# Moving the gate factors, the diagonals and a zeroing in an attention and two-layer MoE kernel

## The chip, the core and the metric

The kernel runs on one core of a Trainium2 chip. The metric is device time in microseconds; the kernel before has a median of 632.36 us over 3 runs (630.68 to 632.56).

## What is computed

Inputs are q, k, v of 2 batches, 8 heads, 576 positions and 64 features, all float32. Three stages follow each other.

```python
# 1. attention with 128 positive random features
phi(x) = exp(x @ omega.T - |x|^2/2 - max) / sqrt(128)
num = phi(q) @ (phi(k).T @ v);  den = phi(q) @ sum(phi(k)) + 1e-6
x = (num / den), heads side by side            # 1152 x 512
# 2. top-1 mixture of 8 experts (512 -> 1024 -> 512)
e_idx = argmax(x @ w_gate);  gate_w = softmax(x @ w_gate)[e_idx]
eom = sigmoid(x @ w_output_gate)
out[row] = gate_w * eom[e_idx] * (relu(x @ w1[e_idx]) @ w2[e_idx])
# 3. dense mixture of 4 experts, weights p = domain_probs / sum
out = sum_e p[:, e] * (relu(out @ w1[e]) @ w2[e])
```

## The kernel before

Float32 products are made of three matmuls each: an operand is split into a rounded high part (a cast on ScalarE, L91) and the remainder (a subtraction, L92, on VectorE or GpSimd), and high x high, high x low and low x high are summed (`mm3`, lines 594 to 596).

*Attention* (lines 506 to 577) is a software pipeline over banks: for each batch b, half hh of the heads, and kind k or q. Stage A transposes (L273), stage B projects into a PSUM bank `pj` (L295 to L297), takes maxima (L300), makes the bias `nb` (L304, L305) and the exponentials `e` (L312, ScalarE). Stage C for k multiplies into `kv` (L326), which shares a PSUM bank with the maxima; for q it transposes `e` (L357). Stage D (`stage_d`, L365) divides (`rd`, `xn`: L377 to L380), writes `xn` to memory for later (L382), transposes (L385) and writes `xh` (ScalarE, L396) and `xl` (VectorE, L397). The tiles of one half are j = 0 to 3 and then the remaining 64 rows.

*Gate.* When a batch's last half is done, `gate_logits` (L400) makes the logits of both gates in two column groups: `lgs` (ScalarE copy, L411) and `lgr`, the 32 remaining columns (VectorE copy, L412). `gate_tr` transposes them (L418); `main_expert` finds the batch's most frequent expert: `gm_eq` (L431), a count matmul (L433), and `ei`. `gate_math` (L449) makes the factors of every row: exponentials on ScalarE (L463, L465) and sixteen small VectorE operations (L459 to L487). `gate_count` (L489) counts rows by expert and chunk with two matmuls and a VectorE sum `cnt`.

*First mixture.* The 1152 rows are four chunks of 288 columns, two a batch. A chunk's main expert is applied to all its rows: layer 1 (`unit1`, eight PSUM tiles `ph`) and layer 2 (`unit2_blocks`, four blocks of 24 matmuls into `py`). A row's factor is zero when its expert is another. The factors come in through `gate_row` (L620): three diagonal pieces `dg` (128x128 twice, 128x32) are spread over partitions by a matmul with ones (L627). The other pairs of expert and chunk that have rows are listed by `extras` (L689); one of them with at most 64 rows is gathered, computed and added in packed form (lines 758 to 848, "the pair": `mask`, `rank`, `og`, `ogf`). Any others would run in a loop (L853). `x2T`, the result, is written by chunks 0 and 1 and added to by chunks 2 and 3, whose columns are therefore zeroed first (L755, GpSimd).

*Second mixture* (lines 885 to 1063) takes the time from about 260 us on: all four experts for all rows, with weights streamed in and split on ScalarE and GpSimd.

*Order.* The program is written in one sequence. A planner then builds each engine's queue from modelled times: whatever is ready and stands earliest in the program goes next. So an instruction can be queued far ahead of its place in the program. On the chip each engine executes its queue in order, and semaphores carry the dependences. `tc.issue_after(ins)` adds an order edge to `ins` for those instructions of its block that run on the same engine as `ins`; instructions on other engines get no edge. Before the change the factors of both batches stand in the program behind layer 1 of chunk 0 (L674), and the planner queues most of batch 0's into the attention of batch 1.

Of the kernel before, what the change touches and what calls it, by code (L numbers as in the profile page):

```python
# [12 lines left out]
AF = mybir.ActivationFunctionType  # L13
ALU = mybir.AluOpType
# [11 lines left out]
NC = 288  # L26
# [14 lines left out]
def moe_stack(ctx, tc, q, k, v, omega, w_gate, w_ogate, mw1, mw2, dprobs, dw1, dw2, out):  # L41
    nc = tc.nc
    TT, STT, TS = nc.vector.tensor_tensor, nc.vector.scalar_tensor_tensor, nc.vector.tensor_scalar

    def f32(ap):
        return ap.bitcast(F32)
# [8 lines left out]
    ps_n = ctx.enter_context(tc.tile_pool(name="ps_n", bufs=2, space=PSUM))  # L55
# [6 lines left out]
    ident = cp.tile([128, 128], F32, name="ident")  # L62
# [13 lines left out]
    fold = cp.tile([128, 32], F32, name="fold")  # L76
# [7 lines left out]
    lgr = cp.tile([16, 128], F32, name="lgr")  # L84
# [280 lines left out]
    def stage_d(b, hh, u):  # L365

        t = st_e["T", u]
        rest = u[1] == 2
        m = 64 if rest else 128
        c0 = 64 * b if rest else 0  # L370
        bank = ps_n.tile([128, 512], F32, tag="nd", name="pnd")
        ps = bank[:, 0:G * (D + 1)].rearrange("p (g d) -> p g d", g=G)
        for i in range(G):
            nc.tensor.matmul(ps[:m, i, :], t[:, i, c0:c0 + m], kvs[b, hh][:, i, :], start=True, stop=True)

        rd = ap.tile([128, G], F32, tag="rd", name="rd", bufs=4)
        TS(rd[:m], ps[:m, :, D], M * 1e-6, None, op0=ALU.add)  # L377
        nc.vector.reciprocal(rd[:m], rd[:m])
        xn = ap.tile([128, G, D], F32, tag="xn", name="xn", bufs=4)
        TT(xn[:m], ps[:m, :, 0:D], rd[:m].unsqueeze(2).to_broadcast([m, G, D]), op=ALU.mult)  # L380
        dst = xs[8, 64 * b:64 * b + 64] if rest else xs[4 * b + SLOT_J[u[3]]]
        nc.sync.dma_start(dst[:, 256 * hh:256 * hh + 256], xn[:m].rearrange("p g d -> p (g d)"))  # L382
        px = bank[:, 0:256].rearrange("p (g n) -> p g n", g=2)
        for g in range(2):
            nc.tensor.transpose(px[:, g, :m], xn[:m, 2 * g:2 * g + 2, :].rearrange("p a d -> p (a d)"), ident[:m, :m])  # L385
        kbs = slice(2 * hh, 2 * hh + 2)
        if rest:
            cols = slice(S * b, S * b + S)
            dh, dl = (z[:, kbs, cols].rearrange("p k (c n) -> p k c n", c=2)[:, :, :, 256:NC] for z in (xh, xl))
            src = px[:, :, 0:64].rearrange("p k (c n) -> p k c n", c=2)  # L390
        else:
            s = SLOT_J[u[3]]
            col = S * b + NC * (s // 2) + 128 * (s % 2)
            dh, dl = (z[:, kbs, col:col + 128] for z in (xh, xl))
            src = px
        nc.scalar.copy(dh, src)  # L396
        TT(dl, src, f32(dh), op=ALU.subtract)  # L397


    def gate_logits(b, psp, tag):  # L400
        lgs = cp.tile([16, 4, 128], F32, tag="lgs", name="lgs")
        for c in range(2):
            ps = psp.tile([16, NC], F32, tag=tag, name="lgp")
            cc = 2 * b + c
            mms = []
            for kb in range(KB):
                for a, x in ((wgh, xh), (wgh, xl), (wgl, xh)):
                    mms.append((a[:, kb, :], x[:, kb, NC * cc:NC * cc + NC]))
            for i, (a, x) in enumerate(mms):
                nc.tensor.matmul(ps, a, x, start=i == 0, stop=i == len(mms) - 1)  # L410
            nc.scalar.copy(lgs[:, 2 * c:2 * c + 2, :], ps[:, 0:256].rearrange("p (t n) -> p t n", n=128))  # L411
            nc.vector.tensor_copy(lgr[:, 32 * cc:32 * cc + 32], ps[:, 256:NC])  # L412
        return lgs

    def gate_tr(b, lgs, psp, tag):
# [33 lines left out]
    def gate_math(b, lg, mx, eq, m, cb):  # L449

        l, z = lg[:, :, 0:NE], lg[:, :, NE:2 * NE]

        def sm(nm, n=NE):
            return cp.tile([128, 5, n] if n > 1 else [128, 5], F32, tag="gm_" + nm, name="gm_" + nm)

        def bc(a):
            return a.unsqueeze(2).to_broadcast([128, 5, NE])

        TS(ohb[:, b], cb, m[:, 0:1], None, op0=ALU.is_equal)  # L459
        d = sm("d")  # L460
        TT(d, l, bc(mx), op=ALU.subtract)
        p = sm("p")
        nc.scalar.activation(p, d, AF.Exp)  # L463
        sg = sm("sg")
        nc.scalar.activation(sg, z, AF.Exp, scale=-1.0)  # L465
        w = sm("w")
        TT(w, eq, rev.unsqueeze(1).to_broadcast([128, 5, NE]), op=ALU.mult)
        wm = sm("wm", 1)
        nc.vector.tensor_reduce(wm, w, axis=AX.X, op=ALU.max)
        oh = sm("oh")  # L470
        TT(oh, w, bc(wm), op=ALU.is_equal)
        ss = sm("ss", 1)
        nc.vector.tensor_reduce(ss, p, axis=AX.X, op=ALU.add)
        TS(ss, ss, 1e-9, None, op0=ALU.add)
        nc.vector.reciprocal(ss, ss)
        TT(p, p, bc(ss), op=ALU.mult)
        TS(sg, sg, 1.0, None, op0=ALU.add)
        nc.vector.reciprocal(sg, sg)
        TT(p, p, sg, op=ALU.mult)
        r = slice(64 * b, 64 * b + 64)  # L480
        nc.vector.tensor_copy(oh_all[:, 4 * b:4 * b + 4, :], oh[:, 0:4])
        TT(g_all[:, 4 * b:4 * b + 4, :], p[:, 0:4], oh[:, 0:4], op=ALU.mult)

        cs = slice(2 * b, 2 * b + 2)
        cm = cmask[:, cs].unsqueeze(2).to_broadcast([128, 2, NE])
        TT(ohr[:, cs], oh[:, 4:5, :].to_broadcast([128, 2, NE]), cm, op=ALU.mult)
        TT(grm[:, cs], p[:, 4:5, :].to_broadcast([128, 2, NE]), ohr[:, cs], op=ALU.mult)  # L487

    def gate_count(b, psp, tag):  # L489
        ps = psp.tile([128, 2, 3, NE], F32, tag=tag, name="cps")  # L490
        nc.tensor.matmul(ps[:, :, 0:2], ones, oh_all[:, 4 * b:4 * b + 4, :].rearrange("p (c t) e -> p c t e", t=2),
                         start=True, stop=True)
        nc.tensor.matmul(ps[:, :, 2], ones, ohr[:, 2 * b:2 * b + 2], start=True, stop=True)
        nc.vector.tensor_reduce(cnt[:, 2 * b:2 * b + 2], ps.rearrange("p c t e -> p c e t"), axis=AX.X, op=ALU.add)
# [25 lines left out]
    gate_late = {}  # L520
# [31 lines left out]
    for st in range(n + LAGD + 2):  # L552
        if st < n:
            kind, b, hh, jp, hp = banks[st]
            if b < 2 and jp == 0 and hp == 0:
                squares(kind, b, hh, nc.vector if (kind, b, hh) == ("k", 0, 0) else nc.gpsimd)
                if kind == "k" and (b, hh) != (0, 0):
                    i = 2 * b + hh + 1
# [61 lines left out]
    def gate_row(s):  # L620

        dg = gp.tile([128, NC], F32, tag="dg", name="dg")
        for t in range(2):
            TS(dg[:, 128 * t:128 * t + 128], ident, s[:, t:t + 1], None, op0=ALU.mult)
        TS(dg[:, 256:NC], fold, s[:, 2:3], None, op0=ALU.mult)
        ps = ps_n.tile([128, NC], F32, tag="nd", name="pg")
        nc.tensor.matmul(ps, ones, dg, start=True, stop=True)  # L627
        g = gp.tile([128, NC], F32, tag="gb", name="gb")
        nc.scalar.copy(g, ps)
        return g  # L630
# [8 lines left out]
    def unit2_blocks(c, w2, hs):  # L639
        gb = gate_row(sel_static(c, c // 2))  # L640
        for d in range(KB):
            y = l2_block(w2, hs, d)
            for dst, src in zip(x2cols(c), (slice(0, 256), slice(256, NC))):
                TT(x2T[:, d, dst], y[:, src], gb[:, src], op=ALU.mult)
            yield

    def unit2(c, w2, hs):
        if c >= 2:
            gb = gate_row(sel_static(c, c // 2))
            return add_out(w2, hs, gb, list(zip(x2cols(c), (slice(0, 256), slice(256, NC)))))  # L650
        for _ in unit2_blocks(c, w2, hs):
            pass

    def x2cols(c):
        return slice(256 * c, 256 * c + 256), slice(1024 + 32 * c, 1056 + 32 * c)
# [15 lines left out]
    E0 = main_weights(0, nc.gpsimd)  # L671
    E0.load1()
    hs = unit1(0, E0.w1, (ps_j, "pj"), (ps_j, "pj"), (ps_j, "pj"), (ps_k, "kv"))
    for b in range(2):  # L674
        gate_math(*gate_late[b])
        gate_count(b, ps_n, "nd")
    pool_a.close()
    yp = ctx.enter_context(tc.tile_pool(name="yp", bufs=1))
    pool_m = ExitStack()
# [67 lines left out]
        return nx, mt, lists[0], lists[1], sel.rearrange("p (c e) -> p c e", c=4), wi  # L747

    E0.load2((nc.vector, nc.gpsimd))
    unit2(0, E0.w2, hs)  # L750
    nx_t, mt, le_t, lc_t, sel1, wi_t = extras()
    hs = unit1(1, E0.w1)
    for c in (2, 3):
        for cols in x2cols(c):
            nc.gpsimd.memset(x2T[:, :, cols], 0.0)  # L755


    pool_x = ExitStack()
    xg_ = pool_x.enter_context(tc.tile_pool(name="xg", bufs=1))
    ex = nc.values_load(wi_t[0:1, 0:1], engines=[SP], min_val=0, max_val=NE - 1)  # L760
# [31 lines left out]
    for t in range(3):  # L792
        TS(og[:, t], slot, rank[:, 0, t:t + 1], mask[:, t:t + 1], op0=ALU.is_equal, op1=ALU.mult)
        for i in range(2):
            TS(ogf[:, t, i], og[:, t], fac[:, t:t + 1], None, op0=ALU.mult)
    px = ps_n.tile([128, KB, SLOTS], F32, tag="nd", name="px")
    for kb in range(KB):
        for t in range(3):
# [41 lines left out]
    blocks = unit2_blocks(1, E0.w2, hs)  # L840
# [252 lines left out]
```

## Time and profile before

| | |
|---|---|
| median of 3 runs | 632.36 us (630.68 to 632.56) |
| profiled execution | 629.91 us |
| its span | 628.1 us |
| mean granted clock of TensorE | 0.988 of full speed |
| TensorE / VectorE / ScalarE / GpSimd busy | 608.2 / 414.1 / 253.9 / 260.3 us |
| HBM read / written | 37.34 / 4.72 MB |

The profile is one execution; times are microseconds from the start of its span. PE is TensorE, DVE VectorE, ACT ScalarE, POOL GpSimd, SPq the DMA issues of SyncE. L412 is line 412 of the kernel. In a timeline a row has start, duration, engine, line, operation, result and operands, count, and in brackets how long the engine had been idle and what released it. In a table by stretches a clock of 1.00 is full speed.

### The profile page before, as it was taken

What the parts mean: (1) busy time and instruction counts of PE and PEld (TensorE: products, weight loads), DVE (VectorE), ACT (ScalarE), POOL (GpSimd) and SP (SyncE); (2) the same over time, 40 slices, a digit from 0 to 9 for tenths busy, and PEclk for the clock granted to TensorE, in tenths of its full rate; (3) what the DMA queues carried; (4) which work ended last, traced back from release to release, by engine and by line L of the source; (5) the groups of instructions that cost most, each with busy time, mean ns of one, the idle gap of its engine ahead of it and who ended that gap; (6) DMA issues with size and microseconds to landing.
All of it is one profiled execution on the core that took longest, in us unless ns stands there. A gap on an engine that the chain in (4) does not pass through costs nothing.

```text
span 628.1 us, 10503 instructions
## 1 busy us (share of the span) xinstructions
PE 608.2 (97%) x3910; PEld 555.7 (88%) x3911; DVE 414.1 (66%) x953; ACT 253.9 (40%) x612; POOL 260.3 (41%) x302
## 2 busy tenths in 40 slices
PE   7999989899999999999999999999999999999996
PEld 6878889799978998799898898898998998998995
DVE  7687685796425388976666666666666666666564
ACT  4566575421304054444343443442442442442230
POOL 4994023310000002367745745745744744744220
PEclk9999997989999999999999999999999999999999
DMA  8632044107335201102202202102201202200004
GB/s 200 160 102 55 22 161 154 32 0 252 99 106 183 87 10 59 67 1 68 68 1 68 68 0 68 68 2 67 68 1 67 68 2 68 67 1 2 2 0 150
DMA packets 41238, 42.77 MB, mean 68 GB/s; under 512 B 14816, under 2 KB 29408, under 8 KB 41184
## 3 DMA queue, kind: packets, MB, share of 16 engines
q1 hardware_dynamic: 40896, 42.00, 21.5%
q8 instruction: 32, 0.52, 0.4%
q14 instruction: 22, 0.18, 0.1%
q10 hardware_dynamic: 288, 0.07, 0.0%
HBM read 37.34 MB, written 4.72 MB: 67 GB/s over the span
## 4 chain that ended last, share of the span: by engine, by line
PE 66%; DVE 3%; issue 0%
PE po L596 10%; PE po L595 10%; PE po L594 10%; PE pp L594 9%; PE pp L596 9%; PE pp L595 9%; PE ph L594 1%; PE py L594 1%; PE py L596 1%; PE ph L595 1%; PE py L595 1%; PE ph L596 1%; DVE xcl L92 1%; DVE c L985 0%; DVE x2T L662 0%
## 5 line engine op out<-in xcount | busy, mean ns | idle before, releaser
L92 POOL TENSOR_TENSOR wlo<-st,whi 128x512 fp32r<-128x512 f32 x100 | 120.8, 1228 | 234.9 <-ACT whi L91 230.6
L1038 DVE SCALAR_TENSOR_TENSOR oacc<-po,pb,oacc 128x512 f32<-128x512 f32 x135 | 100.0, 747 | 55.8 <-PE po L596 55.8
L91 ACT CAST whi<-st 128x512 fp32r<-128x512 f32 x120 | 68.2, 593 | 115.7 <-PE po L596 49.2
L594 PE MATMUL po<-whi,hh 128*128 128x512 f32 x288 | 112.2, 390 | 0.0
L595 PE MATMUL po<-wlo,hh 128*128 128x512 f32 x288 | 112.1, 389 | 0.0
L596 PE MATMUL po<-whi,hl 128*128 128x512 f32 x288 | 111.9, 389 | 0.0
L590 POOL TENSOR_TENSOR hl<-c,hh 128x320 fp32r<-128x320 f32 (+1 forms) x64 | 52.7, 823 | 86.9 <-ACT hh L589 74.3
L594 PE MATMUL pp<-xh,whi 128*128 128x320 f32 (+1 forms) x256 | 75.7, 296 | 0.2 <-DVE u L997 0.2
L596 PE MATMUL pp<-xh,wlo 128*128 128x320 f32 (+1 forms) x256 | 75.8, 296 | 0.0
L595 PE MATMUL pp<-xl,whi 128*128 128x320 f32 (+1 forms) x256 | 75.7, 296 | 0.0
L596 PEld LDWEIGHTS po<-whi,hl 128*128 128x128 f32 x288 | 54.1, 188 | 11.2
L594 PEld LDWEIGHTS po<-whi,hh 128*128 128x128 f32 x288 | 54.1, 188 | 10.1
L595 PEld LDWEIGHTS po<-wlo,hh 128*128 128x128 f32 x288 | 54.1, 188 | 10.0
L985 DVE TENSOR_TENSOR c<-u,pp 128x320 f32<-128x320 f32 (+1 forms) x96 | 43.4, 453 | 22.0 <-PE pp L596 21.6
L594 PEld LDWEIGHTS pp<-xh,whi 128*128 128x128 f32 x256 | 48.5, 190 | 1.7 <-DVE u L997 0.5
L595 PEld LDWEIGHTS pp<-xl,whi 128*128 128x128 f32 x256 | 48.5, 190 | 1.2
L588 ACT ACTIVATE c<-c 128x320 f32<-128x320 f32 (+1 forms) x64 | 28.5, 445 | 51.3 <-DVE c L985 50.5
L596 PEld LDWEIGHTS pp<-xh,wlo 128*128 128x128 f32 x256 | 48.5, 190 | 0.0
L312 ACT ACTIVATE e<-pj,nb 128x128 f32<-128x128 f32 x144 | 41.6, 381 | 14.7 <-DVE nb L305 14.6
L585 DVE SCALAR_TENSOR_TENSOR hl<-c,hh 128x320 fp32r<-128x320 f32 (+1 forms) x64 | 44.9, 735 | 0.2
L594 PE MATMUL ph<-xh,whi 128*128 128x288 f32 x128 | 38.8, 303 | 1.2 <-DVEq L852 1.2
L594 PE MATMUL py<-hh,whi 128*128 128x288 f32 x128 | 39.4, 308 | 0.0
(262 smaller groups left out, 1377.3 us busy)
## 6 DMA issues: line engine op xcount, KB each, us to landing
st<-in_moe_w_dram SPq DMA_DIRECT2D x32, 512.0 KB, 4.3
st<-in_moe_w_dram SPq DMA_DIRECT2D x10, 1024.0 KB, 5.6
v<-in_v_dram SPq DMA_DIRECT2D x16, 128.0 KB, 3.5
q<-in_q_dram SPq DMA_DIRECT2D x4, 512.0 KB, 4.8
xs<-xn SPq DMA_DIRECT2D x16, 128.0 KB, 2.1
own<-in_moe_w_dram SPq DMA_DIRECT2D x2, 1024.0 KB, 5.4
out_dram<-oacc SPq DMA_DIRECT2D x8, 256.0 KB, 2.1
k<-in_k_dram SPq DMA_DIRECT2D x3, 512.0 KB, 4.2
```

The source lines that it names most:

```text
L91: nc.scalar.copy(hi, src)
L92: eng.tensor_tensor(lo, src, f32(hi), op=ALU.subtract)
L312: nc.scalar.activation(e[:, i // 2, i % 2], ps[:, i // 2, i % 2], AF.Exp, bias=nb[:, i // 2, i % 2:i % 2 + 1])
L585: STT(hl, src, 0.0, f32(hh), op0=ALU.max, op1=ALU.subtract)
L588: nc.scalar.activation(c, c, AF.Relu)
L590: nc.gpsimd.tensor_tensor(hl, c, f32(hh), op=ALU.subtract)
L594: nc.tensor.matmul(ps, sh_, mh, start=start, stop=False)
L595: nc.tensor.matmul(ps, sh_, ml, start=False, stop=False)
L596: nc.tensor.matmul(ps, sl_, mh, start=False, stop=stop)
L985: TT(c, u, p, op=op)
L1038: STT(oacc[:, T], po, pc, oacc[:, T], op0=ALU.mult, op1=ALU.add)
```

## The change

The VectorE subtraction that ends a tile in `stage_d` is remembered by tile. Batch 0's `gate_math` and `gate_count` get an order edge behind the subtraction of tile j = 0 of batch 1's second half; batch 1's stand in the program behind the first block of chunk 0's layer 2. The `lgr` copy and the diagonals go from VectorE to ScalarE. The zeroing of `x2T` is written behind the pair's last placement factor.

```diff
@@ stage_d
-        TT(dl, src, f32(dh), op=ALU.subtract)
+        x_done[b, hh, u[1:]] = TT(dl, src, f32(dh), op=ALU.subtract)
+    x_done = {}
@@ gate_logits
-            nc.vector.tensor_copy(lgr[:, 32 * cc:32 * cc + 32], ps[:, 256:NC])
+            nc.scalar.copy(lgr[:, 32 * cc:32 * cc + 32], ps[:, 256:NC])
@@ gate_row
         for t in range(2):
-            TS(dg[:, 128 * t:128 * t + 128], ident, s[:, t:t + 1], None, op0=ALU.mult)
-        TS(dg[:, 256:NC], fold, s[:, 2:3], None, op0=ALU.mult)
+            nc.scalar.activation(dg[:, 128 * t:128 * t + 128], ident, AF.Copy, scale=s[:, t:t + 1])
+        nc.scalar.activation(dg[:, 256:NC], fold, AF.Copy, scale=s[:, 2:3])
@@ behind layer 1 of chunk 0
-    for b in range(2):
-        gate_math(*gate_late[b])
-        gate_count(b, ps_n, "nd")
+    with tc.issue_after(x_done[1, 1, (1, 1, 0)].ins):
+        gate_math(*gate_late[0])
+        gate_count(0, ps_n, "nd")
@@ layer 2 of chunk 0
-    unit2(0, E0.w2, hs)
+    blocks = unit2_blocks(0, E0.w2, hs)
+    next(blocks)
+    gate_math(*gate_late[1])
+    gate_count(1, ps_n, "nd")
+    for _ in blocks:
+        pass
     nx_t, mt, le_t, lc_t, sel1, wi_t = extras()
     hs = unit1(1, E0.w1)
-    for c in (2, 3):
-        for cols in x2cols(c):
-            nc.gpsimd.memset(x2T[:, :, cols], 0.0)
@@ the pair
-            TS(ogf[:, t, i], og[:, t], fac[:, t:t + 1], None, op0=ALU.mult)
+            placed = TS(ogf[:, t, i], og[:, t], fac[:, t:t + 1], None, op0=ALU.mult)
+    with tc.issue_after(placed.ins):
+        for c in (2, 3):
+            for cols in x2cols(c):
+                nc.gpsimd.memset(x2T[:, :, cols], 0.0)
```

## Rows read from the trace of the kernel before

**Rows 1.** The page's engine shares: busy us, share of the span, instructions.

```profile
PE 608.2 (97%) x3910; PEld 555.7 (88%) x3911; DVE 414.1 (66%) x953; ACT 253.9 (40%) x612; POOL 260.3 (41%) x302
```

**Rows 2.** Table by stretches: length, busy time of each engine, clock, DMA share.

```profile
core 0: us, PE busy (x) PEld busy (x) DVE busy (x) ACT busy (x) POOL busy (x), PEclk, DMA share, GB/s
...
92.60:94.00 1.40, 0.17 (x2) 0.07 (x1) 1.40 (x6) 1.05 (x5) 1.40 (x2) 1.00 0.27 90
94.00:102.00 8.00, 8.00 (x44) 7.17 (x45) 3.50 (x13) 3.77 (x12) 4.81 (x4) 0.57 0.51 156
...
122.90:125.00 2.10, 0.25 (x2) 0.12 (x1) 2.10 (x5) 0.41 (x1) 1.00 (x1) 1.00 0.00 0
125.00:129.00 4.00, 4.00 (x19) 3.97 (x20) 3.77 (x12) 2.29 (x6) 1.28 (x1) 0.57 0.00 0
190.00:193.00 3.00, 1.79 (x12) 1.21 (x11) 1.96 (x9) 0.00 (x0) 0.00 (x0) 1.00 0.01 3
249.00:254.00 5.00, 2.88 (x15) 2.00 (x14) 5.00 (x7) 2.07 (x5) 3.97 (x3) 1.00 0.02 7
```

**Rows 3.** Waits of TensorE: total us, times, longest us.

```profile
PE lgt L418 <- DVE lgr L412: 1.9, 1, 1.9
...
PE kv L326 <- DVE nb L305: 1.2, 1, 1.2
```

**Rows 4.** Timeline of VectorE, 92.5 to 94.2.

```profile
92.72 0.18 DVE L378 RECIPROCAL rd<-rd 128x4 f32<-128x4 f32 x1
92.81 1.01 DVE L474 TENSOR_SCALAR gm_ss<-gm_ss 128x5 f32<-128x5 f32 x1
93.73 0.14 DVE L305 SCALAR_TENSOR_TENSOR nb<-sq,kv 128x4 f32<-128x4 f32 x1
```

**Rows 5.** Timeline of GpSimd, 91 to 129.5.

```profile
91.30 3.73 POOL L92 TENSOR_TENSOR wlo<-st,whi 128x512 fp32r<-128x512 f32 x3 [0.56 <-ACT whi L91]
...
118.76 2.07 POOL L755 MEMSET x2T<- 128x1024 f32 x3 [14.29 <-DMA xs<-xn]
...
126.24 1.28 POOL L92 TENSOR_TENSOR wlo<-st,whi 128x512 fp32r<-128x512 f32 x1 [2.34 <-ACT whi L91]
```

**Rows 6.** Timeline of TensorE at two groups of 16 key-value matmuls.

```profile
93.93 2.96 PE L326 MATMUL kv<-v,e 128*128 128x65 f32 x16 [1.23 <-DVE nb L305]
...
102.97 1.89 PE L326 MATMUL kv<-v,e 128*128 128x65 f32 x16
```

**Rows 7.** Timeline of VectorE: diagonals and `lgr`, and diagonals at 192.

```profile
119.61 1.30 DVE L624 TENSOR_SCALAR dg<-ident,sel 128x128 f32<-128x128 f32 x2
...
123.91 0.23 DVE L625 TENSOR_SCALAR dg<-fold,sel 128x32 f32<-128x32 f32 x1
...
124.65 0.17 DVE L412 COPY lgr<-lgp 16x32 f32<-16x32 f32 x1
...
192.18 0.48 DVE L624 TENSOR_SCALAR dg<-ident,sel 128x128 f32<-128x128 f32 x2 [0.61 <-DVEq L852]
```

**Rows 8.** Timeline of ScalarE, 117 to 124.

```profile
117.30 0.27 ACT L396 CAST xh<-pnd 128x128 fp32r<-128x128 f32 x1 [2.10 <-PE pnd L385]
...
120.82 0.36 ACT L411 COPY lgs<-lgp 16x256 f32<-16x256 f32 x1
```

**Rows 9.** Timeline of VectorE: `gm_eq` of batch 0 and of batch 1.

```profile
78.28 0.20 DVE L431 TENSOR_TENSOR gm_eq<-lg,gm_mx 128x40 f32<-128x40 f32 x1
...
126.37 1.21 DVE L431 TENSOR_TENSOR gm_eq<-lg,gm_mx 128x40 f32<-128x40 f32 x1
```

**Rows 10.** The page's groups: the attention's exponentials; busy us, mean ns.

```profile
L312 ACT ACTIVATE e<-pj,nb 128x128 f32<-128x128 f32 x144 | 41.6, 381 | 14.7 <-DVE nb L305 14.6
```

**Rows 11.** Table by stretches: the attention's tail.

```profile
110.00:118.00 8.00, 8.00 (x65) 7.17 (x65) 4.98 (x17) 2.41 (x7) 0.00 (x0) 1.00 0.19 60
```

**Rows 12.** Timelines of VectorE, SyncE and TensorE: counts, the pair's weights, their use.

```profile
134.24 0.21 DVE L494 TENSOR_REDUCE cnt<-cps 128x16 f32<-128x48 f32 x1 [0.24 <-PE cps L493]
...
142.20 1.15 SPq L117 DMA_DIRECT2D st<-in_moe_w_dram  x2
...
165.87 0.88 PE L818 MATMUL phx<-xg,st 128*128 128x64 f32 x6
```

## The prediction

> **What bounds the kernel now.** I read the engine shares first [rows 1]: TensorE is busy 608.2 of 628.1 us, every other engine 414 or less. So time is lost in two ways only: TensorE stands still, or it runs on the lower clock. The waits of TensorE and a table by stretches find both around the change. The wait list has two long ones there [rows 3]: the key-value matmuls of the last attention group wait 1.2 us for VectorE's `nb`, and the gate's transpose (L418) waits 1.9 us for `lgr`. The stretches [rows 2] show what follows each. From 92.6 to 94.0 TensorE is busy 0.17 of 1.40 us, and from 94 to 102 the granted clock averages 0.57, against 1.00 before: most of that stretch is at 1.2 instead of 2.4 GHz. From 122.9 to 125.0 it is busy 0.25 of 2.10, and from 125 to 129 the clock is 0.57 again. Not every standstill does this: 190 to 193 (a branch) is busy 1.79 of 3.00 and 249 to 254 only 2.88 of 5.00, both at 1.00 throughout.
>
> What makes the two waits is read from VectorE's own queue. At 92.81 [rows 4] a division factor of batch 0 (L474, 128x5) takes 1.01 us, while the reciprocal of 128x4 before it takes 0.18; `nb`, which TensorE needs, stands behind it and starts at 93.73. GpSimd is then in weight splits, three from 91.30 to 95.03 [rows 5], so the tiny operation has waited for one of them to end. At 119.61 begin the six diagonal operations of two gate rows [rows 7], the last at 123.91; the same three operations take 0.48 + 0.23 us at 192.18, when GpSimd is idle. Here GpSimd runs zeroing from 118.76 and splits after it [rows 5]. The second `lgr` copy comes only at 124.65, though ScalarE had begun the neighbouring `lgs` copy at 120.82 [rows 8].
>
> **The change, part by part.**
>
> *Batch 0's factors out of the attention.* L474 and its kin may no longer stand ahead of the second-last attention tiles. With L474 gone, `nb` starts at 92.81 instead of 93.73: 0.92 us less standstill of the 1.23 in front of the matmuls at 93.93 [rows 4, 6]; about 0.3 us remains. If that is too short to lower the clock, the stretch from 94 to 102 gains 8.00 x (1 - 0.57) = 3.44 us [rows 2]. Not all of it: 16 key-value matmuls took 2.96 us on the low clock and 1.89 on the high [rows 6], and at 1.89 the eight exponentials that feed them come late: 8 x 0.29 (41.6 us over 144 [rows 10]) = 2.31, so 0.42 comes back as a wait. Term: 3.02, with ends 0 and 3.44.
>
> *Where they go.* Sixteen VectorE operations of 0.14 to 0.40 us now queue behind the first tile of the last group, in a stretch (110 to 118) where VectorE is busy 4.98 of 8.00 [rows 11], and GpSimd not at all. They start about 0.1 us apart, so some 2 us go into 3 us of idle time. Behind them in VectorE's queue stand the tail tiles' normalisations, and behind those TensorE's transposes and the logits; TensorE has chunk 0's layer-1 matmuls as cover, and was busy 8.00 of 8.00 there. I take 0.3 us lost; the ends are 0 and 2.10, the longest stall of ScalarE's in-order queue there [rows 8].
>
> *Diagonals and `lgr` on ScalarE.* VectorE loses the six operations that held `lgr`; `lgr` follows `lgs` on the same queue and is ready by about 121.4, 3.2 us earlier. The wait of 1.85 us (the 1.9 of [rows 3]) goes entirely, and the clock with it: 4.00 x (1 - 0.57) = 1.72 us [rows 2]. ScalarE pays 6 x 0.29, less for the narrow ones: under 1.8 us. These are wanted only by matmul L627, which opens layer 2 of chunk 0 around 134, and ScalarE is busy 2.29 of the 4.00 us from 125 [rows 2], so this is hidden; the two trios at 192 hide the same way. If that cover were gone, 1.8 us would be the price. The two `lgr` copies of batch 0 stand among the exponentials of the attention: between 0 and 2 x 0.36 us (`lgs`, eight times as wide [rows 8]); I take 0.2.
>
> *What is late next.* After the transpose the count matmul L433 needs VectorE's `gm_eq`. That operation took 0.20 us at 78.28 and 1.21 at 126.37, where it ended with a GpSimd split that had begun at 126.24 [rows 5, 9]. Before, the low clock hid this: TensorE crept through the matmuls ahead of L433. At full clock it reaches L433 sooner, so between 0 and 1.01 us of new wait appears; the splits also move earlier, since ScalarE no longer holds their casts while it waits for batch 1's logits. I take the middle, 0.5.
>
> The Trainium skill, page "SBUF — State Buffer", section "Who interferes with whom", speaks to just this: a VectorE instruction with two SBUF inputs contends with a GpSimd instruction that reads SBUF, and the second to issue fully blocks, while ScalarE never waits on anyone. The trace agrees (1.21 beside 0.20), and by that rule taking only the diagonals from VectorE does not free the equality test. By it alone this term would be the full 1.01 and the saving 0.5 us smaller.
>
> *Batch 1's factors behind block 0.* This is program order only, without an order edge: VectorE's part can still be queued early where VectorE is idle. The count matmuls on TensorE do move: 24 matmuls later, some 3 us (65 take 8.00 us in [rows 11]), so `cnt` comes near 137.2 instead of 134.24 [rows 12]. Behind it hangs the chain that picks the pair of few tokens, then SyncE's loads of its expert's weights, issued at 142.20. TensorE uses them at 165.87. Shifted by 3 us the issue still leads by 20 us; cost nothing. The cover is these 20 us; past them, each us late costs one.
>
> *Zeroing x2T.* The zeroing is on GpSimd and the named instruction on VectorE, so the order edge binds nothing; only its place in the program moves. GpSimd is idle from 104.5 until memory comes free at 118.76, so I expect the zeroing to stay there: 0 us. Were it to go to the pair's place, GpSimd is idle there too, and only the first split of the layer-2 weights would come 2 us earlier: 0 again, as those weights are first used in layer 2, around 134.
>
> **Sum.** 0.92 + 3.02 + 1.85 + 1.72 - 0.3 - 0.2 - 0.5 = 6.5 us. Everything behind 130 us is TensorE-bound or chained to it and only shifts. The profiled execution took 629.91 us (span 628.1 and 1.8 around it), so it would take 623.4; the timed runs' median of 632.36 lies 2.45 above it, and carrying the saving over gives 625.9.
>
> **The rivals.**
>
> *The low clock of 94 to 102 stays.* For: the stretch before it already holds small waits, and 0.3 us would still be there. Against: 249 to 254 stands worse and stays at 1.00 [rows 2]. Then 3.02 is not gained: 628.9.
>
> *The equality test becomes the new stop.* By the mechanism above, with the full 1.01 and with the clock falling after it as it did after the 1.85. For: the two rows of 0.20 and 1.21. Against: 1.0 us is less than the 1.21 of 190 to 193, which left the clock alone. Price: 0.5 + 1.72, so 628.1.
>
> *The planner gives the waits back.* Each engine's order is rebuilt from modelled times, and those did not see GpSimd's hold on VectorE. If the transpose is queued that much earlier, the wait at L418 returns with its clock (3.57), and if some other small operation comes before `nb`, most of the first is lost as well (3.02): 632.5, no change.
>
> *Slower: the tail jams.* Place: the sum over batch 0's exponentials (L473) now stands on VectorE in the attention's tail and needs ScalarE's L463, which can queue behind a cast that waits 2.10 us for TensorE (the one at 117.30 [rows 8]). Behind L473 stand the last normalisations, and so the logits. For: VectorE and ScalarE both execute in order, and the stretch is a ping-pong of the three engines. Against: TensorE has matmuls of layer 1 to run. It decides from the point where the hold-up exceeds what is queued ahead of the logits. Price: 2.10, then the low clock as after the first standstill, 3.44, and batch 1's gate late as today, 3.57: 9.1 lost, 635.0.
>
> **How the numbers follow.** Forecast 0.46, the low clock stays 0.20, equality test 0.12, given back 0.12, tail jams 0.10. The likeliest is 625.9; its own range, from the ends of its terms, is 624 to 629. The timed runs spread over 1.9 us, about 0.3%, so below 630.5 counts as faster and above 634.3 as slower. The first three lie below 630.5 but for a few hundredths of each: faster 0.73; same 0.17; slower 0.10. For 8 in 10 the range must take in the first three cases and part of the fourth: 621 to 632.
>
> **What would show it.** First step: no factor operation on VectorE before 110, the wait before the key-value matmuls near 0.3 us, clock 1.00 from 94 to 102. Second: `lgr` right behind `lgs` on ScalarE, no 1.9 us wait at L418, clock 1.00 up to the second unit. Third: a wait of up to 1 us at L433 beside a GpSimd split. Fourth: zeroing still first on GpSimd once memory is free, and the pair's weights issued about 3 us later against the start of layer 2, with no TensorE wait at their use. The prediction is wrong if either low-clock stretch stands, or if TensorE has a new wait of over 1 us between 90 and 140.

## The result, and the profile after

The changed kernel takes 623.99 us (median of 19 runs, 620.54 to 630.72), the kernel before 630.71 (19 runs beside them): a ratio of 0.9893, interval 0.9869 to 0.9918, which is 5.2 to 8.3 us. The ratio and its interval leave out runs that counted as slow, 630.72 us at a mean clock of 0.981 among them. The forecast was 625.9, a saving of 6.5 us; the medians differ by 6.72. Most of the 1.9 us between 625.9 and 623.99 is the base: the kernel before came to 632.36 in 3 runs and to 630.71 in these 19. The profiled execution took 623.27 us, with a span of 621.2, against 629.91 and 628.1. TensorE is still the bound at 97%; some of VectorE's work (414.1 to 407.8 us) has gone to ScalarE [rows 1].

The page's engine shares after (busy us, share of the span, instructions):

```profile
PE 604.8 (97%) x3910; PEld 553.0 (89%) x3911; DVE 407.8 (66%) x937; ACT 257.4 (41%) x628; POOL 259.8 (42%) x302
```

The table by stretches after, at the places of [rows 2] and at the second mixture's start (length, busy time and count of each engine, clock, DMA share, GB/s):

```profile
92.60:94.00 1.40, 1.40 (x13) 1.40 (x13) 0.33 (x1) 1.40 (x5) 1.40 (x2) 1.00 0.41 140
94.00:102.00 8.00, 8.00 (x67) 7.15 (x66) 3.83 (x13) 5.46 (x18) 6.47 (x6) 1.00 0.40 150
...
121.00:125.00 4.00, 4.00 (x33) 4.00 (x32) 4.00 (x14) 3.41 (x12) 1.93 (x2) 1.00 0.00 0
125.00:129.00 4.00, 4.00 (x31) 3.90 (x31) 2.96 (x21) 0.81 (x2) 0.00 (x0) 1.00 0.00 0
...
241.00:245.00 4.00, 2.08 (x13) 1.55 (x12) 4.00 (x5) 2.04 (x5) 2.59 (x2) 1.00 0.00 0
245.00:249.00 4.00, 4.00 (x16) 3.50 (x17) 4.00 (x7) 1.36 (x4) 1.46 (x2) 0.57 0.48 165
```

Both places of [rows 2] are now full of matmuls at 1.00: 67 matmul records stand in 94 to 102, where there were 44. The last row is where a low clock stands now: the low level of 0.57 (most of it at 1.2 instead of 2.4 GHz), which stood at 94 and at 125 before, now stands at 245, behind a standstill of 1.92 us in 241 to 245. That standstill is old (249 to 254 in [rows 2]); there the clock had stayed at 1.00 in this profile.

The timeline of TensorE after: the first of the key-value matmuls [rows 6], the gate's transpose, the count matmul, and the broadcast that opens layer 2. None has a bracket, so none waited:

```profile
92.92 1.90 PE L326 MATMUL kv<-v,e 128*128 128x65 f32 x16
...
118.27 0.23 PE L420 MATMUL lgt<-ident,lgr 16*128 16x16 f32 x1
...
119.92 0.39 PE L435 MATMUL cps<-gm_eq,ones 128*128 128x40 f32 x2
...
126.24 0.73 PE L629 MATMUL pg<-dg,ones 128*128 128x288 f32 x2
```

The timeline of VectorE after. The first factor operation stands at 106.31, behind the subtraction that the order edge names. L476 (L474 before) takes 0.16 us there, not the 1.01 of [rows 4], as GpSimd is idle. The last three are batch 1's, beside GpSimd's splits:

```profile
106.31 0.22 DVE L461 TENSOR_SCALAR ohb<-cb,cbm 128x8 f32<-128x8 f32 x1
...
110.50 0.16 DVE L476 TENSOR_SCALAR gm_ss<-gm_ss 128x5 f32<-128x5 f32 x1
...
119.28 0.49 DVE L433 TENSOR_TENSOR gm_eq<-lg,gm_mx 128x40 f32<-128x40 f32 x1
...
120.89 0.85 DVE L463 TENSOR_TENSOR gm_d<-lg,gm_mx 128x40 f32<-128x40 f32 x1
121.66 1.29 DVE L441 SCALAR_TENSOR_TENSOR cb<-cs,cbm,rev 128x8 f32<-128x8 f32 x1
```

The timeline of ScalarE after: `lgr` directly behind `lgs`, and the diagonals between hidden-layer casts, in the time of [rows 7]:

```profile
116.81 0.36 ACT L413 COPY lgs<-lgp 16x256 f32<-16x256 f32 x1
117.08 0.17 ACT L414 COPY lgr<-lgp 16x32 f32<-16x32 f32 x1
...
121.65 0.69 ACT L626 ACTIVATE dg<-ident,sel 128x128 f32<-128x128 f32 x2
122.23 0.31 ACT L627 ACTIVATE dg<-fold,sel 128x32 f32<-128x32 f32 x1
```

Where the time went is counted with a coarser table of TensorE, first of the kernel before:

```profile
90.00:103.00 13.00, 11.51 (x69) 9.81 (x67) 8.05 (x31) 8.43 (x25) 8.25 (x7) 0.74 0.43 135
...
118.00:136.00 18.00, 16.15 (x108) 14.73 (x108) 15.83 (x63) 7.93 (x19) 7.71 (x8) 0.91 0.00 1
240.00:262.00 22.00, 19.88 (x126) 18.25 (x126) 19.66 (x27) 11.26 (x20) 7.97 (x6) 1.00 0.14 49
```

and of the kernel after:

```profile
90.00:103.00 13.00, 12.61 (x105) 11.53 (x105) 7.30 (x25) 9.93 (x29) 9.94 (x8) 1.00 0.40 127
...
118.00:136.00 18.00, 18.00 (x134) 17.62 (x134) 15.24 (x79) 6.40 (x19) 4.26 (x5) 1.00 0.01 2
240.00:262.00 22.00, 20.08 (x110) 17.87 (x109) 21.90 (x34) 10.94 (x23) 7.87 (x7) 0.92 0.14 49
```

Standstill in the first two rows was 1.49 + 1.85 = 3.34 us and is 0.39: 2.95 gained. The clock cost 13.00 x 0.26 + 18.00 x 0.09 = 5.00 and costs nothing. That makes 7.95 on paper. Followed by instruction the gain is less: the pair's first matmul comes 7.13 us earlier (165.87 in [rows 12], 158.74 below), the matmul behind the longer wait at the second mixture's start 7.28 (252.11 to 244.83), and the end 6.9. That wait is the same 1.23 us in both kernels, before and after:

```profile
252.11 0.41 PE L594 MATMUL pp<-xch,whi 128*128 128x320 f32 x1 [1.23 <-DVE c L985]
```

```profile
244.83 0.41 PE L596 MATMUL pp<-xch,whi 128*128 128x320 f32 x1 [1.23 <-DVE c L991]
```

In 240 to 262 the clock takes 22.00 x 0.08 = 1.76 on paper, but from this wait to the end only 0.4 us are lost.

### The profile page after: what moved, and what is told of

It is laid out like the page before. It is cut to its first block, busy times and chain, and to the rows that moved or that the text cites. A ratio compares the mean times of both kernels' runs of the same rounds, so it can differ in the third digit from the quotient of the medians.

```text
span 621.2 us, 10506 instructions
## 1 busy us (share of the span) xinstructions
PE 604.8 (97%) x3910; PEld 553.0 (89%) x3911; DVE 407.8 (66%) x937; ACT 257.4 (41%) x628; POOL 259.8 (42%) x302
## 4 chain that ended last, share of the span: by engine, by line
PE 68%; DVE 1%; issue 0%; ACT 0%; ACTq 0%
PE po L597 11%; PE po L596 11%; PE po L598 11%; PE pp L596 9%; PE pp L598 9%; PE pp L597 9%; PE ph L596 1%; PE py L596 1%; PE py L598 1%; PE ph L598 1%; PE ph L597 1%; PE py L597 1%; DVE xcl L92 0%; DVE x2T L664 0%; DVE xl L92 0%; PE pg L629 0%
## 5 line engine op out<-in xcount | busy, mean ns | idle before, releaser
L596 PE MATMUL pp<-xch,whi 128*128 128x320 f32 (+1 forms) x128 | 38.1, 298 | 1.2 <-DVE c L991 1.2
```

Source lines behind the costliest of these rows:

```text
L596: nc.tensor.matmul(ps, sh_, mh, start=start, stop=False)
```

## The experiments

Line numbers are those of each kernel's own trace. The first four each do a part of the change alone.

**Batch 0's order edge alone.**

```diff
-        TT(dl, src, f32(dh), op=ALU.subtract)
+        x_done[b, hh, u[1:]] = TT(dl, src, f32(dh), op=ALU.subtract)
...
-    for b in range(2):
-        gate_math(*gate_late[b])
-        gate_count(b, ps_n, "nd")
+    with tc.issue_after(x_done[1, 1, (1, 1, 0)].ins):
+        gate_math(*gate_late[0])
+        gate_count(0, ps_n, "nd")
+    gate_math(*gate_late[1])
+    gate_count(1, ps_n, "nd")
```

> The kernel before, with only batch 0's factors queued behind the attention's first tail tile. Theory of the prediction (each half removes one TensorE wait and the low clock behind it): no L474-like operation before the key-value matmuls near 93, that wait falls from 1.2 to 0.4 us or less, clock 1.00 from 94 to 102, and the transpose's wait on lgr stays at 1.9 us: 3.4 us faster (3.0 to 4.2), ratio 0.9945. Rival (only the diagonals matter): less than 1 us, ratio 0.999. Rival (the standstills matter, the low clock comes by chance whatever is removed): 0.9 us, ratio 0.9985.

Measured: 627.29 us against 630.81, ratio 0.9946, interval 0.9916 to 0.9976. The table by stretches and the waits of TensorE (total us, times, longest us):

```profile
94.00:102.00 8.00, 8.00 (x68) 7.26 (x68) 3.83 (x13) 5.93 (x19) 7.29 (x6) 1.00 0.49 174
122.00:128.00 6.00, 5.97 (x33) 5.65 (x34) 5.38 (x20) 2.84 (x7) 2.57 (x2) 0.72 0.00 0
```

```profile
PE lgt L420 <- DVE lgr L414: 1.8, 1, 1.8
```

The first stop and its low clock are gone, the second stands as before with the clock at 0.72 behind it: this half is worth 3.5 us.

**`lgr` and the diagonals on ScalarE, without the edges.** The edit is the diff's hunks of `gate_logits` and `gate_row`.

> The kernel before, with only the diagonals and lgr on ScalarE. Theory of the prediction: the 1.9 us wait for lgr goes, with the low clock behind it, and the 1.2 us wait of the key-value matmuls stays unless the attention is queued anew: 3.1 us faster (2.4 to 3.6), ratio 0.995. Rival (only the diagonals matter): 6.5 us, ratio 0.9897. Rival (the low clock comes by chance): 1.6 us, ratio 0.9975.

Measured: 628.07 against 630.81, ratio 0.9953, interval 0.992 to 0.9987. The size is the expected one, the way to it is not. Timeline of VectorE and the longest new wait of TensorE:

```profile
100.39 1.29 DVE L500 TENSOR_TENSOR selt<-grm,ohb 128x8 f32<-128x8 f32 x1
```

```profile
PE pnd L374 <- DVE xl L397: 2.7, 2, 2.3
```

With `lgr` off VectorE, the planner put batch 0's factors earlier in VectorE's queue. The addition of 1e-9 now ran at 81.86 in 0.16 us, GpSimd being idle, so the first wait vanished without an edge. But four of the last factors came to be held beside the splits, took 0.9 to 1.3 us each, and stopped TensorE for 2.3 us a little later; the clock of 102 to 106 is 0.57.

**The diagonals alone on ScalarE** (the hunk of `gate_row`).

> The kernel before, with only the diagonals on ScalarE; lgr stays on VectorE, behind two weight splits. Theory of the prediction: the six diagonal operations were what held lgr, so its wait shrinks from 1.9 to 0.5 us or less: 2.9 us faster (2.0 to 3.6), ratio 0.9954. Rival (lgr's place on ScalarE is what counts): the wait stays over 1 us, gain under 1 us.

Measured: 628.08 against 630.81, ratio 0.9953, interval 0.9925 to 0.9982. The table by stretches:

```profile
94.00:102.00 8.00, 8.00 (x46) 7.05 (x45) 3.60 (x16) 4.06 (x13) 4.34 (x4) 0.57 0.44 156
118.00:130.00 12.00, 11.42 (x84) 10.16 (x82) 10.38 (x40) 8.83 (x23) 7.52 (x8) 1.00 0.00 1
```

This is the other half, clean: the low clock at 94 stays, the stop at 123 and its low clock are gone. The diagonals were what held `lgr`. Behind them the forecast's third wait came out: `gm_eq` took 1.05 us (123.91 to 124.96, a split ends at 124.89), and TensorE waited 0.58 us for it, with the clock at 1.00:

```profile
125.10 0.39 PE L433 MATMUL cps<-gm_eq,ones 128*128 128x40 f32 x2 [0.58 <-DVE gm_d L461]
```

**`lgr` alone on ScalarE** (the hunk of `gate_logits`).

> The kernel before, with only lgr on ScalarE; the six diagonal operations stay on VectorE beside GpSimd. Theory of the prediction: the transpose no longer waits for lgr, but gm_eq now stands behind the diagonals on VectorE, so the same 1 to 2 us appear at the count matmul L433: gain under 1.5 us, ratio 0.998 to 1.0. Rival (lgr's place is what counts): 3.1 us faster, ratio 0.995.

Measured: 626.83 against 630.81, ratio 0.9934, interval 0.9901 to 0.9967: a miss, as it gained 4.0 us; the rival's 3.1 is nearer. Waits of TensorE, and the first diagonals on VectorE:

```profile
PE cps L433 <- DVE gm_d L461: 2.0, 1, 2.0
```

```profile
117.12 2.35 DVE L624 TENSOR_SCALAR dg<-ident,sel 128x128 f32<-128x128 f32 x2 [0.66 <-DMA xs<-xn]
```

What was expected at the gate did happen: the wait only moved from the transpose to the count matmul, 2.0 us, since VectorE still makes the diagonals first. What was not expected is that the factors of batch 0 were queued anew here too (the addition at 78.80, 0.16 us), which took the 1.2 us wait for `nb` away; four of the factors left over ran at 93 to 98 in 0.9 to 1.3 us each. Its profile is not free of either low clock: it stands at 0.79 in 94 to 102, behind a wait of 0.93 us for exponentials, and at 0.79 in 122 to 130. That profiled execution is only 1.6 us shorter than that of before, and the runs spread from 623.40 to 631.87. Part of the 2.4 us that their median gains beyond it is the clock: 0.987 in the profiled execution, 0.99 in the median of the 12. The rest stays open.

**One small operation before `nb`.** In two kernels the changed version gets one more 128x5 operation in front of one `nb` of the attention's last groups: an addition of a constant, or a reciprocal.

```diff
...
+            with tc.issue_after(first.ins):
+                tiny = TS(tin, tin, 1e-9, None, op0=ALU.add)     # or reciprocal(tin, tin)
+            with tc.issue_after(tiny.ins):
                 STT(nb, s, -hs, mx, op0=ALU.mult, op1=ALU.subtract)
```

> The kernel after, with one operation added on VectorE, a 128x5 addition of a constant on a tile of its own, between L304 and the bias nb that stands in front of the key-value matmuls near 93. GpSimd is in four weight splits from 90.5 to 95.5 there. Theory (a small operation of this form waits for a GpSimd split to end, and TensorE waits behind it): it takes about 1.0 us and not 0.16, the matmuls wait 0.6 to 1.2 us, and part of the executions fall to the low clock: 1 to 4 us slower than the kernel after, ratio to before 0.990 to 0.996. Rival (the operations of the factors cost only their own time): 0.2 us, ratio 0.989.

> As the run before it, but the added operation is a reciprocal of 128x5, a form that took 0.18 us beside a GpSimd split. Theory: 0.2 us, no wait over 0.5 us in front of the key-value matmuls, ratio to before 0.989 to 0.990. Rival (any operation there costs as much, since VectorE's queue is full): as slow as the constant's addition.

Measured: 625.82 (ratio 0.9895, 0.9865 to 0.9925) with the addition and 622.93 (0.986, 0.9838 to 0.9882) with the reciprocal. The operation itself, in the one trace and in the other:

```profile
94.49 1.20 DVE L310 TENSOR_SCALAR tin<-tin 128x5 f32<-128x5 f32 x1
```

```profile
91.33 0.18 DVE L310 RECIPROCAL tin<-tin 128x5 f32<-128x5 f32 x1
```

Both ran beside splits of GpSimd (four from 93.16 to 98.12 in the one, eight from 90.00 to 99.91 in the other). The same size, the same place in the program, 1.20 against 0.18 us: it is the kind of operation that is held, not whatever stands there. The times do not bear out what was expected of them: with the addition it was the rival's 0.989 and not 0.990 to 0.996, and with the reciprocal 0.986, below the 0.989 to 0.990 expected. Though 2.9 us apart, they are no clean measure of the operation: the extra operation re-ordered the rest, TensorE waits only 0.5 us for the delayed `nb` and another 0.6 us at the count matmul in the addition's kernel, and the clock stayed at 1.00 in 94 to 102 with both. The low clock that follows the stop in the kernel before was not brought back by this.

**Batch 1's factors put back before layer 2**, and **the zeroing put behind the splits**, each taken from the changed kernel:

```diff
-    next(blocks)
-    gate_math(*gate_late[1])
...
-                nc.gpsimd.memset(x2T[:, :, cols], 0.0)
+                tc.keep_in_program_order(nc.gpsimd.memset(x2T[:, :, cols], 0.0))
```

> The kernel after, with batch 1's factors at their old place, behind layer 1 of chunk 0. Theory (this part of the change is worth nothing): ratio to before 0.988 to 0.991, no TensorE wait over 0.6 us from 110 to 140, the pair's weights issued 3 us earlier. Rival (their place matters, because batch 1's exponentials hold ScalarE's queue while they wait for the logits): 1 us or more lost, ratio 0.991 to 0.995.

> The kernel after, with the zeroing of x2T queued on GpSimd behind its last weight split of the layer-2 weights. Theory (the zeroing's place is worth nothing, since VectorE's diagonals have left): splits 2 us earlier, zeroing near 121, ratio to before 0.988 to 0.991. Rival (the zeroing still delays splits that layer 2 or the gate waits for): 0.5 to 1 us faster than the kernel after, ratio 0.987 to 0.988.

Measured: 624.3 (0.9899, 0.9872 to 0.9925) and 625.1 (0.9894, 0.987 to 0.9918), the same as the change. In the first the pair's weights were issued 3.7 us earlier (135.37) and TensorE had no new wait over 0.2 us. In the second, GpSimd's timeline shows that the zeroing really moved, from 114.77 to:

```profile
124.10 2.15 POOL L801 MEMSET x2T<- 128x1024 f32 x4
```

The splits did not come 2 us earlier for it, as was expected: the first stands at 117.22, and at 116.72 in the changed kernel. Neither part carries the gain.

**The layer-2 splits of the second mixture later.** An attempt to do better by the same reasoning:

```diff
-        nc.scalar.copy(hh, c)
+        hid_cast.append(nc.scalar.copy(hh, c))
...
+            if w2 is None:
+                with tc.issue_after(hid_cast[0].ins):
+                    w2 = load_w2(e, j)
...
```

> The change as it is, and the first layer-2 weights of the second mixture are split behind the first hidden block's cast. In the changed kernel two pairs of GpSimd splits (238.16 to 240.7 and 242.41 to 245.5) lie beside VectorE's chain that prepares the second mixture's inputs (1.63, 2.28 and 2.64 us, beside 0.53, 1.22 and about 1.3 without a split), and TensorE waits 0.70 and 1.23 us for it. Theory (two-input VectorE work stands still beside splits, here too): the chain is some 2.9 us shorter, both waits go, and the low clock at 245 to 249 with them: 1.5 to 2.5 us less than the changed kernel, a ratio to the kernel before of 0.985 to 0.987. Rival (the splits only move onto the next two-input operations, the hidden blocks' low halves): no gain, 0.989 to 0.990, with a TensorE wait of the same length in 246 to 252. Against both: layer 2's weights come too late, over 0.992.

Measured: 624.72 (0.9908, 0.9874 to 0.9942), no gain; the rival was right in kind, if not in its numbers (0.989 to 0.990, a wait in 246 to 252). Timeline of VectorE and the waits of TensorE there:

```profile
239.92 1.23 DVE L92 TENSOR_TENSOR xl<-x2T,xh 128x1024 fp32r<-128x1024 f32 x1 [1.02 <-ACT xh L91]
...
248.78 3.10 DVE L587 SCALAR_TENSOR_TENSOR hl<-c,hh 128x320 fp32r<-128x320 f32 x2
```

```profile
247.11 0.50 PE L599 MATMUL po<-wlo,hh 128*128 128x512 f32 x1 [0.78 <-POOL wlo L92]
...
255.97 0.43 PE L598 MATMUL pp<-xdh,whi 128*128 128x320 f32 x1 [2.09 <-DVE c L993]
```

The chain did get faster (1.23 us where the changed kernel takes 2.28), and the waits of 0.7 and 1.2 went. But the splits now ran from 245.32 to 251.5, beside the low halves of the hidden layer, and TensorE stood 0.78 + 2.09 us instead of 1.92. The low clock moved with the standstill: 1.00 from 245 to 255, 0.66 from 255 to 260.

**The two kernels again, unaltered.**

> The changed kernel unaltered, as the other side of the comparison with the later splits, and for a second profile. If the low clock at 245 to 249 belongs to this kernel's standstills there, it is there again (0.5 to 0.8); if it differs from execution to execution, the waits of 0.7 and 1.2 us return and the clock may stay at 1.00. Time: a ratio to the kernel before of 0.988 to 0.991.

> The kernel before, unaltered, for a second profile. Theory (the two standstills at 93 and 123 lower the clock in this kernel): both waits (1.2 and 1.9 us) and both low stretches (94 to 102 and 125 to 129, about 0.57) are there again, within 1 us of their places. Rival (the low clock comes or stays away by chance): the waits are there and at least one of the stretches is at 1.00.

Measured: 622.9 for the change (0.9888, 0.9855 to 0.9921; profiled span 619.2) and, for the kernel before, 631.48 in one run. The table by stretches of the second profile of before:

```profile
92.60:94.00 1.40, 0.34 (x3) 0.10 (x2) 1.25 (x5) 1.19 (x5) 1.40 (x3) 1.00 0.29 97
94.00:102.00 8.00, 7.84 (x41) 7.19 (x41) 3.73 (x15) 3.68 (x10) 5.04 (x5) 0.57 0.48 156
...
125.00:129.00 4.00, 3.73 (x18) 3.69 (x19) 3.94 (x12) 1.56 (x4) 1.28 (x1) 0.57 0.00 0
254.00:260.00 6.00, 5.81 (x27) 5.41 (x27) 6.00 (x12) 2.43 (x6) 1.95 (x2) 0.72 0.55 175
```

Both stops and both low stretches are there again, to the microsecond. The stretch behind 254 is different: 0.72 here, 1.00 in the first profile. The changed kernel's second profile again has the low clock there (0.57 from 243 to 247). It is not the change that brings it. The same two waits, 0.7 and 1.2 us, stand at this place in thirteen profiles, all but that of the later splits. In the 6 us behind the second one the clock is 0.72 or 0.73 in eight of them (both of the change, the second of before, and those of the order edge, of ScalarE's part, of the two small operations and of the zeroing), and 1.00 in five (the first of before, and those of the diagonals, of `lgr`, of batch 1's factors put back and of the experiment that follows).

**The addition of 1e-9 taken away from the kernel before.**

```diff
-        TS(ss, ss, 1e-9, None, op0=ALU.add)
```

> The kernel before without L474, the addition of 1e-9 to the gate's sums; nothing else is changed. Theory (this one operation, 1.01 us beside a split, makes the first stop): the wait of the key-value matmuls for nb and the low clock at 94 to 102 are gone, the wait at L418 stays: 3.4 us less than the kernel before, a ratio of 0.993 to 0.996. Rival (the reciprocal or another factor operation behind it takes its place before nb): the wait stays, 0.999 to 1.001.

Measured: 633.54 against 630.6, ratio 1.0058, interval 1.002 to 1.0096: slower, which neither theory expected. Timeline of VectorE, and of TensorE:

```profile
93.68 0.16 DVE L474 RECIPROCAL gm_ss<-gm_ss 128x5 f32<-128x5 f32 x1
93.76 0.12 DVE L305 SCALAR_TENSOR_TENSOR nb<-sq,kv 128x4 f32<-128x4 f32 x1
...
94.81 1.16 DVE L475 TENSOR_TENSOR gm_p<-gm_p,gm_ss 128x40 f32<-128x40 f32 x1
...
96.20 1.18 DVE L480 COPY oh_all<-gm_oh 128x32 f32<-128x32 f32 x1
```

```profile
99.90 0.33 PE L385 MATMUL pnd<-ident,xn 64*128 64x64 f32 x2 [1.10 <-DVE xn L380]
102.50 2.68 PE L326 MATMUL kv<-v,e 128*128 128x65 f32 x16 [0.53 <-DVE nb L305]
...
129.15 0.23 PE L418 MATMUL lgt<-ident,lgr 16*128 16x16 f32 x1 [1.99 <-DVE lgr L412]
```

This profile runs 0.87 us later than that of before up to the place in question: the reciprocal `rd` stands at 93.59, at 92.72 in [rows 4]. From it to `nb` it is 0.17 us here and was 1.01 there: the factors' reciprocal now in between costs 0.16. The wait for `nb` at this place is gone, so the addition was the first stop's cause; 0.65 us of TensorE, a wait for the exponentials, came in its stead. But taking the addition out lets the rest of the factors run on beside the splits, those shown for 1.16 and 1.18 us, and TensorE stops 1.10 and 0.53 us some microseconds later, with a low clock (0.70, then 0.50) in 102 to 110. The gain comes from moving the whole sequence to where GpSimd is idle.

The last row shows something else. It is the second stop, 1.99 us where it was 1.85, and this time the clock stays at 1.00 behind it:

```profile
129.20:133.00 3.80, 3.80 (x29) 3.77 (x30) 3.80 (x12) 2.52 (x7) 2.00 (x2) 1.00 0.00 0
```

So a standstill of this length does not bring the low clock each time. The other way round it holds: in every profile in which one of the two stops is gone and no other wait of 0.9 us or more came in its stead, the clock is 1.00 at that place.

## Why the prediction was right

*The first stop.* Right in place and mechanism: the edge alone gained 3.5 us, where the two terms gave 0.92 + 3.02 = 3.94. Of the wait nothing is left, where 0.3 us was forecast. What comes in its stead is 0.39 us of TensorE in front of the projection at 92.59, a wait for the exponentials.

*The queue's new place.* The 0.3 us for the tail was not spent: TensorE is busy 14.00 of 14.00 us from 102 to 116. The factors begin at 106.31 and not behind 110, as the whole stretch had moved up. The slower rival, a jam in the tail, did not occur.

*Diagonals and `lgr`.* Right: no wait at the transpose, clock 1.00 behind it. `lgr` ends at 117.25, directly behind `lgs`. The diagonals take 0.69 + 0.31 us a trio on ScalarE, and the last is done at 124.38, 1.9 us before the broadcast at 126.24. The cover was there, but thinner than the time around 134 suggested, as everything had moved up. Batch 0's two `lgr` copies did not cost their 0.2 us: TensorE stands still 0.13 us from 70 to 90, before it was 0.41.

*The equality test.* This is the term that was wrong: 0.5 us forecast, 0 found. `gm_eq` took 0.49 instead of 0.20 us, held until a split ended at 119.72, and the count matmul followed at 119.92 without a wait. The operations behind it were held longer (0.85 and 1.29 us), but nobody waited for them. The mechanism is real, as the diagonals alone showed (1.05 us held, 0.58 us waited); that the split ended soon behind the start of `gm_eq` here is luck. The Trainium skill, page "SBUF — State Buffer", section "Who interferes with whom", says that a VectorE instruction with two SBUF inputs contends with one of GpSimd that reads SBUF, and that whichever is issued second is blocked: 0.85 and 1.29 us agree. It could not say which of the held operations TensorE would wait for, and the full 1.01 us that the forecast drew from it did not come.

*Batch 1's factors and the zeroing.* Right that both are free. `cnt` came 3.9 us later than before against the start of layer 2 (134.24 to 130.71, while layer 2 moved from 134.06 to 126.60; 3 were forecast), and the pair's weights were issued 4.0 later against their use, still 19.7 us ahead. The zeroing stayed first on GpSimd. The timelines of GpSimd, SyncE and TensorE after:

```profile
114.77 1.99 POOL L801 MEMSET x2T<- 128x1024 f32 x3 [13.59 <-DVE sel L504]
```

```profile
139.03 1.15 SPq L117 DMA_DIRECT2D st<-in_moe_w_dram  x2
```

```profile
158.74 1.44 PE L824 MATMUL phx<-xg,st 128*128 128x64 f32 x11
```

*The sum.* 6.5 forecast, 6.9 in the profiled spans, but the parts differ. Up to 136 us the tables above count 7.95: 2.95 of standstill where the terms gave 0.92 + 1.85 - 0.3 - 0.2 - 0.5 = 1.77, and 5.00 of clock where they gave 4.74. Followed by instruction it was 7.28 us at the second mixture's start, 0.8 more than forecast, and 0.4 of them were lost behind it. "Everything behind 130 us only shifts" was too simple: the standstill at the second mixture's start was followed by the low clock this time. That 6.9 lies so near 6.5 is partly luck: two profiles of one kernel are 1.4 us apart (628.1 and 629.5) and 2.0 (621.2 and 619.2). And the forecast's own range of 624 to 629 does not follow from the ends of its terms: as stated they save 0.66 to 7.93 us, which gives 624.4 to 631.7.

*An argument that fell.* Against its first rival the prediction held that 249 to 254 stands worse and keeps its clock. In the second profile of the same kernel it does not. The rival was rightly thought unlikely, but that row was one execution's. In the same way the second stop, whose low clock the forecast counted at 1.72 us, kept 1.00 behind it in the kernel without the addition.

*How much of the gain is clock* is best read from the timed runs, since each has its mean clock. At a mean clock of 0.993 to 0.995 the change's span is 621.8 us (median of 9) and that of before 626.1 (of 6): 4.3 us with the clock alike. The median clock rose from 0.988 (62 executions) to 0.994 (25), which leaves some 2.4 us of 6.7 for it. That is half of the 4.74 forecast. Why is open: the timed runs have no table by stretches, and which executions of either kernel ran low behind the stops at 93 and 123, or at the second mixture's start, no record shows.

*The parts together.* 3.5 for the edge and 2.7 for ScalarE's part make 6.2, near the whole. That they add is partly luck: without the edge, moving `lgr` re-orders the factors too, so ScalarE's part alone removed both old waits and made a new one.

## What to carry to other kernels

When a tiny operation sits in front of the bound engine, look at what GpSimd does at that moment: here a VectorE operation of 0.16 us cost 1.0 beside a split, and moving the whole sequence into a stretch without splits gained 3.5 us, where removing that one operation lost 2.9. A standstill is worth more than its length where the low clock follows it, but take from several profiles whether it follows each time. An edit that frees one engine re-orders that engine's queue elsewhere, so read the whole stretch, not only the place that was edited.

## What the runs showed of the hardware that was not expected

Beside GpSimd's splits a 128x5 addition of a constant on VectorE took 1.20 us and a 128x5 reciprocal 0.18; a copy of 128x32 took 1.18, a reciprocal of 128x40 0.39. The `nb` operation, with two inputs and 128x4, took 0.12 to 0.15 there. By the kernel only one of its inputs, `sq`, lies in SBUF, the other, `kv`, in PSUM; the operations with two inputs that were held (`gm_eq`, `gm_d`, `cb`, `gm_p`, `selt`: 0.49 to 1.31 us) read both from SBUF. No run changed the place of an input alone. Why the addition and the copy, with one input, are held and the reciprocals are not was not settled.

The same two waits of TensorE, 0.7 and 1.2 us within 3 us, were followed by a granted clock of 1.00 in one profile of the kernel before and by 0.72 in another, and over thirteen profiles by the low clock in eight. The two stops at 93 and 123 were followed by 0.57 in both profiles of the kernel before, but a stop of 1.99 us at the second place by 1.00 in another kernel.
